# Grouping the batch loads and giving them more buffers in a fused attention, Fourier and gated MLP kernel

## The chip, the core and the metric

The kernel runs on one core of one Trainium2 chip. The metric is the device time of one execution in microseconds (us), as a median over several runs. A core has five engines that run side by side and meet through semaphores: PE (TensorE, matrix multiply, with PEld for its weight loads), DVE (VectorE), ACT (ScalarE), POOL (GpSimd) and SP (SyncE, which in this kernel issues every DMA).

## What is computed

The reference is three layers one after the other, for a batch of 4, a sequence of 1088 and a model width of 128 (4 heads of 32). Everything is in float32.

```python
# 1. linear attention with 64 product features per head
a, b = S1 @ x, S2 @ x                      # 8 + 8 numbers for each token and head, for x = q and x = k
phi = outer(a, b)                          # 64 features
kv, z = sum_s phi(k) v, sum_s phi(k)
attn = (phi(q) @ kv) / (phi(q) @ z + 1e-6)
# 2. Fourier mixing and a channel MLP
u = x + real(fft(fft(x, axis=seq), axis=feature))
x2 = u + relu(layernorm(u) @ w_ch1) @ w_ch2
# 3. a spatial gating unit
h = relu(x2 @ w_in); gate, v = halves of h
out = (gate * (w_spatial @ layernorm(v) + b_spatial)) @ w_out
```

The spatial product is the large one: a 1088 x 1088 matrix by 1088 x 512 in each of the 4 batches. The kernel gets float32 accuracy out of it by splitting both operands into a high and a low part, so that each product is three matmuls.

## The kernel before, in words

The program is written with a framework that takes the source as a list of operations with a priority, follows tiles and their buffers, and fixes an order for each engine at compile time. Operations that stand later in the source can therefore be put ahead of earlier ones on their engine, wherever the framework's own model has them ready first. At run time each engine follows its fixed order and waits on semaphores.

Each batch goes through these stages, and each stage has a function of its own:

- `keys(b)` (L355) handles the keys in three chunks of 384 tokens. For each chunk it loads the value tile `vx` (L359, 128 x 396 floats, 198 KB) and calls `feats`, then multiplies features by values into `kv` (L365), which ACT copies out to `kvz`.
- `feats` (L336) loads a chunk of transposed keys or queries (`kt` or `qt`, L338, 128 x 384 floats, 192 KB, both in the tag `kq` with 6 buffers), multiplies it by the projection `sb_s` on PE (L341, tile `abp`), copies that to `ab` on ACT (L343, 2 buffers) and forms the products of features `pp` on DVE (L347, 3 buffers of 128 x 768 floats).
- `queries(b)` (L376) does `feats` for three chunks of queries, transposes the products on PE (L386, tile `qps`, which needs the permutation tile `prm`), copies them to `qp` on ACT (L391), multiplies them by `kvz` on PE (L397, tile `nm`) and divides on DVE into `ub` (L405 to L407).
- `fourier_seq(b)` (L414) and `fourier_feat(b)` (L475) add the real part of the two-dimensional transform to `ub`. They need the tables `tr` (1096 KB), `trr` (137 KB) and `dd` (256 KB).
- `channel(b)` (L165) is the channel MLP and the first half of the gating unit, which leaves the normalised `v` as `vh` and `vlo` for the spatial product.
- `spatial(b)` (L570) is the spatial product (tile `ac`, L589 to L591) and the output.

The weights arrive in double precision, as ten blocks of 256 KB (`wraw`, L328): two each of w1, w2 and wo and four of wi. `weight` (L331) converts each with five DVE, four ACT and two POOL instructions. The spatial weights (`wst`, L126) come in strips of 192 KB and pass through buffers that are shared with later tiles. `warm(n)` (L505) issues n matmuls of zeros whose place in PE's order is fixed: 11 at the start, 10 early in the Fourier stage of batch 0 and 20 ahead of `channel(0)`.

The order of the loads in the source is, before the change: `sb_s`; then for batch 0 the pairs `vx`, `kt` of the three chunks; `prm`; four weight blocks (wi 0 and 1, wo 0 and 1; L526); the three `qt`; six weight blocks (w1, w2, wi 2 and 3; L528); `tr`, `trr`, `dd` (L531 to L533); the pairs of batch 1 and its `qt`; the spatial strips. The loads of batch 2 and batch 3 stand inside `keys` and `queries` in the loop at L556, behind the strips of the first two column blocks of the spatial weights.

Of the kernel before, what the change touches and what calls it, by code (L numbers as in the profile page):

```python
# [7 lines left out]
F32 = mybir.dt.float32  # L8
# [10 lines left out]
P = 128  # L19
# [46 lines left out]
def fourier_attention_gmlp_kernel(  # L66
# [18 lines left out]
    nc = tc.nc  # L85
# [8 lines left out]
    prm = const.tile([P, 3, P], F32, name="prm")  # L94
# [193 lines left out]
    ca = sa.enter_context(tc.tile_pool(name="ca", bufs=1, side="right"))  # L288
# [3 lines left out]
    tr = ca.tile([P, 2, 4, NCOL], F32, name="tr")  # L292
    trr = ca.tile([P, NCOL], F32, name="trr")
    dd = ca.tile([P, 2, 2, DM], F32, name="dd")
# [5 lines left out]
    def xtile(b, shape, name):  # L300
        if b == 0 and name not in ("abp", "nm"):
            return psy.tile(shape, F32, tag="acc", bufs=2, name=name)
        return psx.tile(shape, F32, tag="x", bufs=3, name=name)
# [21 lines left out]
    def weight_load(tag, *blocks):  # L325
        t = const.tile([P, len(blocks), 512], I32, tag=tag, name="wraw")
        for i, (n, src, k) in enumerate(blocks):
            nc.sync.dma_start(out=t[:, i, :], in_=src.bitcast(I32)[:, 512 * k:512 * k + 512])  # L328
            wraw[n, k] = t[:, i, :]

    def weight(n, k):  # L331
        w_ = from_f64(wraw.pop((n, k)), 256, None, False)
        A.copy(out=wt[n][:, k, 0, :], in_=w_)
        sub(G, wt[n][:, k, 1, :], w_, wt[n][:, k, 0, :])

    def feats(src, b, c, tag):  # L336
        x = ca.tile([P, 384], F32, tag="kq", bufs=6, name=tag)
        nc.sync.dma_start(out=x, in_=src[b, :, 384 * c:384 * c + 384])  # L338
        ap = xtile(b, [P, 2, 3, 32], "abp")
        for t in range(3):  # L340
            mm(out=ap[:, :, t, :], lhsT=x[:, 128 * t:128 * t + 128], rhs=sb_s, start=True, stop=True)  # L341
        ab = ca.tile([P, 2, 3, 32], F32, tag="ab", bufs=2, name="ab")
        A.copy(out=ab, in_=ap)  # L343
        pp = ca.tile([P, 12, 8, 8], F32, tag="pp", bufs=3, name="pp")
        a_ = ab[:, 0, :, :].rearrange("p t (h i) -> p (t h) i", h=4)
        b_ = ab[:, 1, :, :].rearrange("p t (h j) -> p (t h) j", h=4)
        (G if [b, tag[0], c] in [[3, 'k', 2]] else V).tensor_tensor(  # L347
            out=pp,
            in0=a_.unsqueeze(3).to_broadcast([P, 12, 8, 8]),
            in1=b_.unsqueeze(2).to_broadcast([P, 12, 8, 8]),  # L350
            op=ALU.mult,
        )
        return pp

    def keys(b):  # L355
        kv = psx.tile([P, 512], F32, tag="y", name="kv")[:, 0:66].rearrange("p (r d) -> p r d", r=2)
        for c in range(3):
            vx = ca.tile([P, 3, 4, 33], F32, tag="vx", bufs=3, name="vx")
            nc.sync.dma_start(out=vx, in_=vt[b, :, 3 * c:3 * c + 3, :, :])  # L359
            pp = feats(kT, b, c, "kt")  # L360
            for t in range(3):
                for pr in range(2):
                    for hh in range(2):
                        h = 2 * pr + hh
                        mm(  # L365
                            out=kv[64 * hh:64 * hh + 64, pr, :],
                            lhsT=pp[:, 4 * t + h, :, :].rearrange("p i j -> p (i j)"),
                            rhs=vx[:, t, h, :],
                            start=(c == 0 and t == 0 and pr == 0),
                            stop=(c == 2 and t == 2 and pr == 1),  # L370
                        )
        z = kvz[b % 2]
        A.copy(out=z[0:64, :, 0:33], in_=kv[0:64])
        A.copy(out=z[64:128, :, 33:66], in_=kv[64:128])

    def queries(b):  # L376
        z = kvz[b % 2]
        ub[b] = const.tile([P, NT, DM], F32, tag="ub", bufs=3, name="ub")
        qps = []
        for c in range(3):  # L380
            pp = feats(qT, b, c, "qt").rearrange("p t i j -> p (t i j)")
            qp = ca.tile([P, 2, 384], F32, tag="qp", bufs=3, name="qp")
            for pr in range(2):
                q_ = xtile(b, [P, 384], "qps")
                for t in range(3):
                    T.transpose(  # L386
                        out=q_[:, 128 * t:128 * t + 128],
                        in_=pp[:, 256 * t + 128 * pr:256 * t + 128 * pr + 128],
                        identity=ident,
                    )  # L390
                A.copy(out=qp[:, pr, :], in_=q_)  # L391
            qps.append(qp)
        for c, qp in enumerate(qps):
            nm = xtile(b, [P, 3, 4, 33], "nm")
            for t in range(3):
                for pr in range(2):
                    mm(  # L397
                        out=nm[:, t, 2 * pr:2 * pr + 2, :].rearrange("p h d -> p (h d)"),
                        lhsT=qp[:, pr, 128 * t:128 * t + 128],
                        rhs=z[:, pr, :],  # L400
                        start=True,
                        stop=True,
                    )
            rd = ca.tile([P, 3, 4, 1], F32, tag="rd", bufs=2, name="rd")
            V.tensor_scalar(out=rd, in0=nm[:, :, :, 32:33], scalar1=1e-6, scalar2=None, op0=ALU.add)  # L405
            V.reciprocal(out=rd, in_=rd)
            V.tensor_tensor(  # L407
                out=ub[b][:, 3 * c:3 * c + 3, :].rearrange("p t (h d) -> p t h d", h=4),
                in0=nm[:, :, :, 0:32],
                in1=rd.to_broadcast([P, 3, 4, 32]),  # L410
                op=ALU.mult,
            )
# [106 lines left out]
    blocks = [("w1", 0), ("w1", 1), ("w2", 0), ("w2", 1), ("wi", 2), ("wi", 3), ("wi", 0), ("wi", 1), ("wo", 0), ("wo", 1)]  # L519
    srcs = {"w1": w1, "w2": w2, "wi": win, "wo": wout}  # L520
    def load_raw(tag, part):
        weight_load(tag, *[(n, srcs[n], k) for n, k in part])

    keys(0)
    nc.sync.dma_start(out=prm, in_=perm)
    load_raw("wsh0", blocks[6:])  # L526
    queries(0)
    load_raw("wsl0", blocks[:6])  # L528
    weight("w1", 0)
    weight("w1", 1)  # L530
    nc.sync.dma_start(out=tr, in_=trig)  # L531
    nc.sync.dma_start(out=trr, in_=trig_r)
    nc.sync.dma_start(out=dd, in_=ddft)  # L533
    fourier_seq(0)
    fourier_feat(0)
    weight("wi", 2)
# [9 lines left out]
    for _ in channel(0, pre, psy, "acc", 2, psy, "o", None, [convert(("w2", 0), ("w2", 1), ("wo", 0), ("wo", 1)), None, None, None, convert(("wi", 0), ("wi", 1)), None]):  # L546
        pass
    keys(1)
    queries(1)
    with tc.issue_after(marks[0, 1, "t1"].ins):  # L550
        spatial_split(pre, 0, [G], spatial_load(const, 0, ring))
    sp.close()
# [2 lines left out]
    spatial_split(ca, 1, (V, G), spatial_load(pw, 1, ring))  # L555
    for b in range(1, B):  # L556
        if b > 1:
            keys(b)
            queries(b)
        fourier_seq(b)  # L560
        fourier_feat(b)
# [174 lines left out]
```

## Time and profile before

| | us |
|---|---|
| median of 3 runs | 468.57 |
| lowest and highest run | 465.99 and 468.98 |
| the profiled execution, whole | 467.55 |
| the profiled execution, its span | 465.7 |
| PE busy in the span | 444.4 |
| DVE busy in the span | 276.3 |
| ACT busy in the span | 192.3 |
| POOL busy in the span | 65.5 |

The span runs from the first to the last instruction that the profiler recorded; 1.85 us of the execution lie around it. Busy times are sums over the whole span, and the stages differ: the first 100 us hold the attention, the Fourier transform and the channel MLP of batch 0 and all weight conversions, and from then on PE also has the spatial product to work on. All matmuls are pipelined, so a PE that counts as busy can still be working slowly, at a lower granted clock or with short matmuls.

### The profile page before, as it was taken

The numbers are of one execution on the slowest core, as the hardware profiler recorded it, in microseconds if no ns is written. First come the engines' busy times: TensorE is split into PE (matmuls) and PEld (weight loads), VectorE is DVE, ScalarE is ACT, GpSimd is POOL, SyncE is SP. The second block draws the span as 40 slices with busy tenths as digits, with TensorE's granted clock in tenths as the row PEclk, the third lists the DMA queues.
The fourth block names the chain that finished last, engine by engine and source line by source line (L and its number), as shares of the span: only waits on it lengthen the run. The fifth ranks groups of instructions, "written<-read, shape, count | busy, mean of one in ns | idle before, by whom it ended". The sixth has DMA issues, their size and how long they took to land.

```text
span 465.7 us, 7498 instructions
## 1 busy us (share of the span) xinstructions
PE 444.4 (95%) x2893; PEld 410.0 (88%) x2893; DVE 276.3 (59%) x685; ACT 192.3 (41%) x448; POOL 65.5 (14%) x105
## 2 busy tenths in 40 slices
PE   8968898989999998999999999999999999999996
PEld 7847777868979788889999999999999999999995
DVE  3589998896564484878736273784454547221221
ACT  3546687464223153555524242563333335312221
POOL 2045394471100130000000000000000000000000
PEclk9799799999999998999999999999999999999999
DMA  8961143004000040000000000000000000000000
GB/s 245 374 205 34 35 121 106 16 19 129 27 1 1 2 144 1 0 1 18 16 1 0 1 17 1 18 1 14 1 1 18 0 2 18 14 1 17 1 17 15
DMA packets 13007, 19.29 MB, mean 41 GB/s; under 512 B 1446, under 2 KB 11436, under 8 KB 12844
## 3 DMA queue, kind: packets, MB, share of 16 engines
q1 hardware_dynamic: 12972, 18.82, 12.7%
q8 instruction: 23, 0.38, 0.3%
q14 instruction: 12, 0.10, 0.1%
HBM read 16.58 MB, written 2.23 MB: 40 GB/s over the span
## 4 chain that ended last, share of the span: by engine, by line
PE 71%; issue 9%; DVE 7%; ACT 5%; POOL 3%; DMA 3%; SPq 1%; POOLq 0%; DVEq 0%; ACTq 0%
PE ac L590 12%; PE ac L591 12%; PE ac L589 12%; PE v_ps L256 2%; PE dft L451 2%; PE v_ps L254 2%; PE c L227 2%; PE v_ps L255 2%; PE ac L597 1%; PE ac L596 1%; PE u_ps L582 1%; PE c L225 1%; PE u_ps L583 1%; PE u_ps L584 1%; PE c L226 1%
## 5 line engine op out<-in xcount | busy, mean ns | idle before, releaser
L589 PE MATMUL ac<-wsh,vh 128*128 128x384 f32 (+1 forms) x384 | 126.9, 331 | 0.6 <-ACT vh L270 0.6
L590 PE MATMUL ac<-wsl,vh 128*128 128x384 f32 (+1 forms) x384 | 126.9, 330 | 0.0
L591 PE MATMUL ac<-wsh,vlo 128*128 128x384 f32 (+1 forms) x384 | 126.6, 330 | 0.0
L590 PEld LDWEIGHTS ac<-wsl,vh 128*128 128x128 f32 x384 | 72.4, 189 | 1.8 <-issue 1.0
L589 PEld LDWEIGHTS ac<-wsh,vh 128*128 128x128 f32 x384 | 72.3, 188 | 1.6 <-ACT vh L270 0.9
L591 PEld LDWEIGHTS ac<-wsh,vlo 128*128 128x128 f32 x384 | 72.4, 188 | 0.9 <-issue 0.4
L600 DVE TENSOR_TENSOR uh<-ac,uh 128x384 f32<-128x384 f32 (+1 forms) x48 | 25.4, 530 | 55.3 <-PE ac L597 55.3
L586 ACT ACTIVATE uh<-u_ps 128x384 f32<-128x384 f32 (+1 forms) x48 | 22.6, 470 | 47.7 <-PE u_ps L584 45.0
L347 DVE TENSOR_TENSOR pp<-ab 128x768 f32<-128x768 f32 x23 | 25.2, 1108 | 18.9 <-ACT ab L343 17.6
L114 DVE TENSOR_TENSOR gl<-uh,gh 128x384 fp32r<-128x384 f32 (+1 forms) x48 | 26.2, 547 | 13.4 <-ACT gh L601 13.3
L245 POOL CAST xh<-xh 128x64 fp32r<-128x64 f32 x4 | 2.2, 541 | 202.7 <-ACT xh L242 202.7
L601 ACT CAST gh<-uh 128x384 fp32r<-128x384 f32 (+1 forms) x48 | 23.5, 492 | 15.0 <-DVE uh L600 14.8
L261 DVE BATCH_NORM_STATS2 bst<-vn 128x6 f32<-128x512 f32 x27 | 18.6, 693 | 16.8 <-ACT vn L259 16.7
L259 ACT ACTIVATE vn<-v_ps 128x512 f32<-128x512 f32 x27 | 16.0, 598 | 19.2 <-PE v_ps L256 18.7
L241 DVE TENSOR_TENSOR xt<-c,xt 128x384 f32<-128x384 f32 (+1 forms) x12 | 6.4, 532 | 27.8 <-PE c L227 27.8
L397 PE MATMUL nm<-kvz,qp 128*128 128x66 f32 x144 | 17.4, 278 | 0.0
L397 PEld LDWEIGHTS nm<-kvz,qp 128*128 128x128 f32 x144 | 17.3, 198 | 0.0
L282 ACT CAST vh<-vn 128x1024 fp32r<-128x1024 f32 x12 | 12.6, 1047 | 10.3 <-PE ac L590 8.2
L227 PE MATMUL c<-hl,w 128*128 128x384 f32 (+1 forms) x48 | 16.4, 342 | 0.3 <-DVE hl L220 0.3
L225 PE MATMUL c<-hh,w 128*128 128x384 f32 (+1 forms) x48 | 16.6, 346 | 0.0
L256 PE MATMUL v_ps<-wi,xl 128*128 128x512 f32 x36 | 15.3, 425 | 1.1 <-DVE xl L114 1.1
L582 PE MATMUL u_ps<-sxh,wi 128*128 128x384 f32 (+1 forms) x48 | 16.2, 338 | 0.0
(714 smaller groups left out, 950.2 us busy)
## 6 DMA issues: line engine op xcount, KB each, us to landing
wst<-in_wsp SPq DMA_DIRECT2D x18, 192.0 KB, 3.3
vx<-in_vt SPq DMA_DIRECT2D x12, 198.0 KB, 4.1
kt<-in_kT SPq DMA_DIRECT2D x12, 192.0 KB, 3.8
qt<-in_qT SPq DMA_DIRECT2D x12, 192.0 KB, 4.1
w2st<-in_wsp SPq DMA_DIRECT2D x9, 160.0 KB, 3.3
tr<-in_trig SPq DMA_DIRECT2D x1, 1096.0 KB, 8.9
wraw<-in_win SPq DMA_DIRECT2D x4, 256.0 KB, 5.4
wraw<-in_w SPq DMA_DIRECT2D x4, 256.0 KB, 4.8
```

Source lines behind the costliest of these rows:

```text
L114: eng.tensor_tensor(out=lo, in0=x, in1=hi.bitcast(F32), op=ALU.subtract)
L225: mm(out=c2[:, 0:n], lhsT=wpart("w2", 0, 128 * m, 128), rhs=hh[:, 0:n], start=(m == 0), stop=False)
L227: mm(out=c2[:, 0:n], lhsT=wpart("w2", 0, 128 * m, 128), rhs=hl[:, 0:n], start=False, stop=(m == 3))
L256: mm(out=h_, lhsT=xl[:, cs], rhs=wt["wi"][:, 2:4, 0, :], start=False, stop=True)
L347: (G if [b, tag[0], c] in [[3, 'k', 2]] else V).tensor_tensor(out=pp, in0=a_.unsqueeze(3).to_broadcast([P, 12, 8, 8]), in1=b_.unsqueeze(2) ...
L397: mm(out=nm[:, t, 2 * pr:2 * pr + 2, :].rearrange("p h d -> p (h d)"), lhsT=qp[:, pr, 128 * t:128 * t + 128], rhs=z[:, pr, :], start=True, ...
L586: A.activation(out=uh[:, 0:n], in_=h_[:, 0:n], func=ACTF.Relu)
L589: mm(out=ac[:, 0:n], lhsT=vh[:, k, ms], rhs=wsh[c][:, k, :], start=(k == 0), stop=False)
L590: mm(out=ac[:, 0:n], lhsT=vh[:, k, ms], rhs=wsl[c][:, k, :], start=False, stop=False)
L591: mm(out=ac[:, 0:n], lhsT=vl[:, k, ms], rhs=wsh[c][:, k, :], start=False, stop=False)
L600: V.tensor_tensor(out=uh[:, 0:n], in0=ac[:, 0:n], in1=uh[:, 0:n], op=ALU.mult)
L601: A.copy(out=gh[:, 0:n], in_=uh[:, 0:n])
```

## The change

All loads of a batch are taken out of `keys` and `feats` and put into a function `loads(b)`, which issues three `kt`, three `qt` and three `vx` in that order (for batch 0 with `prm` after the `kt`). `loads(0)` stands ahead of everything else, then come `tr`, `trr`, the six weight blocks w1, w2, wi 2 and 3, then `dd`, `loads(1)`, and last the four weight blocks wi 0 and 1, wo 0 and 1. `loads(2)` is moved ahead of the strips of the spatial weights, and `loads(3)` stands at the head of batch 3. The tag `kq` gets 10 buffers instead of 6, `vx` 5 instead of 3, and `pp` 4 instead of 3. The memory reserved by the `dynamic_dma_scratch_size` of the program goes from 4096 to 1024.

```diff
--- before.py
+++ after.py
@@ -333,15 +333,27 @@
         A.copy(out=wt[n][:, k, 0, :], in_=w_)
         sub(G, wt[n][:, k, 1, :], w_, wt[n][:, k, 0, :])
 
-    def feats(src, b, c, tag):
-        x = ca.tile([P, 384], F32, tag="kq", bufs=6, name=tag)
-        nc.sync.dma_start(out=x, in_=src[b, :, 384 * c:384 * c + 384])
+    loaded = {}
+
+    def loads(b):
+        for tag, src in (("kt", kT), ("qt", qT)):
+            for c in range(3):
+                x = loaded[b, tag, c] = ca.tile([P, 384], F32, tag="kq", bufs=10, name=tag)
+                nc.sync.dma_start(out=x, in_=src[b, :, 384 * c:384 * c + 384])
+            if b == 0 and tag == "kt":
+                nc.sync.dma_start(out=prm, in_=perm)
+        for c in range(3):
+            vx = loaded[b, "vx", c] = ca.tile([P, 3, 4, 33], F32, tag="vx", bufs=5, name="vx")
+            nc.sync.dma_start(out=vx, in_=vt[b, :, 3 * c:3 * c + 3, :, :])
+
+    def feats(b, c, tag):
+        x = loaded.pop((b, tag, c))
         ap = xtile(b, [P, 2, 3, 32], "abp")
         for t in range(3):
             mm(out=ap[:, :, t, :], lhsT=x[:, 128 * t:128 * t + 128], rhs=sb_s, start=True, stop=True)
         ab = ca.tile([P, 2, 3, 32], F32, tag="ab", bufs=2, name="ab")
         A.copy(out=ab, in_=ap)
-        pp = ca.tile([P, 12, 8, 8], F32, tag="pp", bufs=3, name="pp")
+        pp = ca.tile([P, 12, 8, 8], F32, tag="pp", bufs=4, name="pp")
         a_ = ab[:, 0, :, :].rearrange("p t (h i) -> p (t h) i", h=4)
         b_ = ab[:, 1, :, :].rearrange("p t (h j) -> p (t h) j", h=4)
         (G if [b, tag[0], c] in [[3, 'k', 2]] else V).tensor_tensor(
@@ -355,9 +367,8 @@
     def keys(b):
         kv = psx.tile([P, 512], F32, tag="y", name="kv")[:, 0:66].rearrange("p (r d) -> p r d", r=2)
         for c in range(3):
-            vx = ca.tile([P, 3, 4, 33], F32, tag="vx", bufs=3, name="vx")
-            nc.sync.dma_start(out=vx, in_=vt[b, :, 3 * c:3 * c + 3, :, :])
-            pp = feats(kT, b, c, "kt")
+            vx = loaded.pop((b, "vx", c))
+            pp = feats(b, c, "kt")
             for t in range(3):
                 for pr in range(2):
                     for hh in range(2):
@@ -378,7 +389,7 @@
         ub[b] = const.tile([P, NT, DM], F32, tag="ub", bufs=3, name="ub")
         qps = []
         for c in range(3):
-            pp = feats(qT, b, c, "qt").rearrange("p t i j -> p (t i j)")
+            pp = feats(b, c, "qt").rearrange("p t i j -> p (t i j)")
             qp = ca.tile([P, 2, 384], F32, tag="qp", bufs=3, name="qp")
             for pr in range(2):
                 q_ = xtile(b, [P, 384], "qps")
@@ -521,16 +532,17 @@
     def load_raw(tag, part):
         weight_load(tag, *[(n, srcs[n], k) for n, k in part])
 
+    loads(0)
+    nc.sync.dma_start(out=tr, in_=trig)
+    nc.sync.dma_start(out=trr, in_=trig_r)
+    load_raw("wsl0", blocks[:6])
+    nc.sync.dma_start(out=dd, in_=ddft)
+    loads(1)
+    load_raw("wsh0", blocks[6:])
     keys(0)
-    nc.sync.dma_start(out=prm, in_=perm)
-    load_raw("wsh0", blocks[6:])
     queries(0)
-    load_raw("wsl0", blocks[:6])
     weight("w1", 0)
     weight("w1", 1)
-    nc.sync.dma_start(out=tr, in_=trig)
-    nc.sync.dma_start(out=trr, in_=trig_r)
-    nc.sync.dma_start(out=dd, in_=ddft)
     fourier_seq(0)
     fourier_feat(0)
     weight("wi", 2)
@@ -547,6 +559,7 @@
         pass
     keys(1)
     queries(1)
+    loads(2)
     with tc.issue_after(marks[0, 1, "t1"].ins):
         spatial_split(pre, 0, [G], spatial_load(const, 0, ring))
     sp.close()
@@ -555,6 +568,8 @@
     spatial_split(ca, 1, (V, G), spatial_load(pw, 1, ring))
     for b in range(1, B):
         if b > 1:
+            if b > 2:
+                loads(b)
             keys(b)
             queries(b)
         fourier_seq(b)
@@ -719,7 +734,7 @@
     import concourse.bacc as bacc
     from concourse.bass_utils import run_bass_kernel_spmd
 
-    nc = bacc.Bacc("TRN2", target_bir_lowering=False, num_devices=1, dynamic_dma_scratch_size=4096)
+    nc = bacc.Bacc("TRN2", target_bir_lowering=False, num_devices=1, dynamic_dma_scratch_size=1024)
     lay = _layout(**{n: np.asarray(x) for n, x in inputs.items()})
     arrays, args = {}, []
     for n in _INS:
```

## Rows read from the trace of the kernel before

**Rows 1.** The page: busy time of PE and DVE in the span.
```profile
PE 444.4 (95%) x2893; PEld 410.0 (88%) x2893; DVE 276.3 (59%) x685; ACT 192.3 (41%) x448; POOL 65.5 (14%) x105
```

**Rows 2.** Windows: length, busy us (instructions) of PE, PEld, DVE, ACT, POOL; clock, DMA, GB/s.
```profile
26.00:60.00 34.00, 28.27 (x170) 22.30 (x170) 31.99 (x94) 20.54 (x51) 17.09 (x27) 0.90 0.24 79
60.00:88.00 28.00, 25.86 (x195) 22.11 (x194) 24.07 (x53) 19.56 (x46) 18.99 (x18) 1.00 0.34 94
88.00:180.00 92.00, 87.43 (x688) 74.38 (x688) 60.85 (x141) 34.09 (x85) 22.52 (x40) 0.98 0.14 41
180.00:466.00 286.00, 281.41 (x1670) 271.69 (x1668) 146.71 (x362) 107.32 (x239) 2.21 (x6) 1.00 0.02 8
```

**Rows 3.** The chain that ended last, its start: start us, length us, what.
```profile
2.59 4.22 DMA kt<-in_kT
6.82 5.74 DMA qt<-in_qT
12.70 3.46 PE abp L341 x18
```

**Rows 4.** Timeline of SP (DMA issues): start us, us spent issuing, engine, line, what, count.
```profile
4.49 0.91 SPq L328 DMA_DIRECT2D wraw<-in_win  x2
5.44 1.21 SPq L328 DMA_DIRECT2D wraw<-in_wout  x2
6.82 1.51 SPq L338 DMA_DIRECT2D qt<-in_qT  x3
...
13.01 0.36 SPq L531 DMA_DIRECT2D tr<-in_trig  x1
...
21.96 0.33 SPq L338 DMA_DIRECT2D kt<-in_kT  x1
...
73.59 7.16 SPq L338 DMA_DIRECT2D qt<-in_qT  x2
```

**Rows 5.** Waits of SP's own queue: who waited for whom, us in total, times, longest.
```profile
SPq L338 <- DMA tr<-in_trig: 4.0, 1, 4.0
```

**Rows 6.** Windows of the first 20 us, columns as in rows 2.
```profile
0.00:4.00 4.00, 2.43 (x6) 1.95 (x7) 1.77 (x11) 2.44 (x5) 3.19 (x13) 1.00 0.50 128
4.00:8.00 4.00, 3.96 (x20) 3.24 (x18) 0.48 (x2) 0.35 (x2) 0.00 (x0) 1.00 0.92 270
8.00:12.00 4.00, 3.29 (x78) 3.02 (x78) 2.35 (x3) 1.02 (x4) 0.00 (x0) 1.00 1.02 351
12.00:14.00 2.00, 1.30 (x9) 1.33 (x10) 0.01 (x1) 0.32 (x1) 0.00 (x0) 0.84 1.06 404
14.00:20.00 6.00, 6.00 (x31) 5.67 (x31) 4.74 (x11) 3.46 (x9) 0.00 (x0) 0.50 1.00 384
```

**Rows 7.** Timeline of DVE: start us, busy us, what, count [idle before <- released by].
```profile
7.65 2.70 DVE L347 TENSOR_TENSOR pp<-ab 128x768 f32<-128x768 f32 x3 [3.52 <-ACT ab L343]
13.99 0.96 DVE L347 TENSOR_TENSOR pp<-ab 128x768 f32<-128x768 f32 x1 [3.64 <-ACT ab L343]
...
16.55 0.96 DVE L347 TENSOR_TENSOR pp<-ab 128x768 f32<-128x768 f32 x1 [0.32 <-ACT ab L343]
...
24.49 1.01 DVE L407 TENSOR_TENSOR ub<-nm,rd 128x384 f32<-128x384 f32 x2
```

**Rows 8.** Timeline of PE: the warming matmuls, first projections, first spatial products.
```profile
1.57 5.06 PE L508 MATMUL wp<-a 128*128 128x512 f32 x11 [1.57 <-DVE a L503]
6.43 0.83 PE L341 MATMUL abp<-sb_s,kt 128*128 128x64 f32 x6
...
20.64 3.46 PE L397 MATMUL nm<-kvz,qp 128*128 128x66 f32 x30
...
86.75 0.42 PE L589 MATMUL ac<-wsh,vh 128*128 128x384 f32 x1
```

**Rows 9.** Timeline of DVE, as rows 7: a feature product of batch 1, then batch 2's first.
```profile
59.22 1.77 DVE L347 TENSOR_TENSOR pp<-ab 128x768 f32<-128x768 f32 x1
...
107.51 2.80 DVE L347 TENSOR_TENSOR pp<-ab 128x768 f32<-128x768 f32 x3
```

## The prediction

> **What bounds the kernel now.** Start with the page's busy times. PE is busy for 444.4 of 465.7 us, DVE for 276.3 [rows 1], so PE looks like the limit, with at most 21 us to win. The windows by stage show where those 21 us lie [rows 2]: from 180 us on PE idles for 4.6 of 286 us, between 88 and 180 us for 4.6 of 92. No load order helps there. Between 26 and 60 us it is DVE that is full, 31.99 of 34 us, and PE idles for 5.7; between 60 and 88 us DVE is busy for 24.1 of 28. In these two stages batch 0 goes through the Fourier transform and the channel MLP beside the weight conversions, and at their end, at 86.75 us, the spatial product begins to run in earnest [rows 8], which then fills every gap of PE. So the kernel is a start-up of some 87 us, then PE's sum. A microsecond taken out of the start-up should come out of the total, because the work behind it stays the same.
>
> Read next the start of the chain of waits [rows 3]. Its links up to 12.7 us are two transfers: a key chunk that lands at 6.81 and a query chunk that lands at 12.56 us. SP's timeline tells why the second is so late [rows 4]: four weight blocks (1 MB) were put into the queue at 4.49 to 6.65 us, ahead of the queries at 6.82. DVE shows what that costs [rows 7]: it finishes the three feature products of the keys at 10.35 us, then idles 3.64 us until those of the queries start at 13.99. These should follow at once; instead they end at 17.51, and `ub` is complete at 25.50.
>
> **When the loads land after the change.** The windows of the first 20 us give the rate [rows 6]: 0.51 MB (millions of bytes) have moved by 4 us, 1.59 by 8, 3.00 by 12, 3.80 by 14. Two known landings set the delay behind this curve [rows 3]. The second key chunk ends 0.86 MB of the queue, which the curve reaches at 5.3 us; it landed at 6.81. The first query chunk ends 2.71 MB, reached at 11.2 us; it landed at 12.56. So I add 1.5 us. In the new order the last `kt` ends 0.66 MB, the last `qt` 1.44, the last `vx` 2.05, `tr` 3.17 and the second w1 block 3.84 MB. That gives landings at 6.0, 8.9, 10.8, 13.9 and 15.6 us. The same bytes go through the same queue; only their order changes.
>
> **The keys: nothing won, nothing lost.** Their projections cannot start before PE has run its 11 warming matmuls, whose place is fixed and which last until 6.63 us; the first starts at 6.43 already today [rows 8]. So the key products still run from about 7.65 to 10.35. The values come later than before, at 9.5 to 10.8 us, but `kv` is needed only when the first transposed queries are ready, after 12 us. Bounds: nothing, to 0.8 us if PE's order puts the last `kv` group ahead of a query projection.
>
> **The queries: 4.3 us won.** With `qt` on chip at 8.9 us and a fourth `pp` buffer (the second query product takes over the first key chunk's buffer, which `kv` frees at about 10.3), the three query products follow the keys on DVE: 10.35 plus 3 x 0.96 is 13.2 us, against 17.51 [rows 7]. From the last product to the complete `ub` it took 25.50 - 17.51 = 8.0 us. I keep those 8.0 us, so `ub` is ready at 21.2, 4.3 us earlier. For the tail the bounds are wide: the clock was at 0.50 between 14 and 20 us [rows 6], that is at 1.2 instead of 2.4 GHz, and it had fallen after 12 to 14 us, where PE had worked only 1.30 of 2 us while it waited for `qt`. At full clock 30 of the 36 `nm` matmuls took 3.46 us [rows 8], so all 36 take 4.2; started when the first queries are transposed, at about 12.8, they end at 17.0, and 1.2 us of division makes `ub` complete at 18.2, a gain of 7.3. With all 36 at half clock they take 8.3 and `ub` comes at 22.3, a gain of 3.2. The 8.0 us that were measured lie nearer to the second.
>
> **Transformation tables and weights: 0.** `tr` is needed at the start of the transform, now about 24 us, and lands at 13.9. The w1 blocks land by 15.6, ahead of the end of the queries. The late weight blocks and the loads of batch 1 are held up in another way. A `kt` load waited 4.0 us on `tr` [rows 5], and it was the eighth DMA behind `tr` (issued at 21.96 [rows 4], when `tr` had just landed). So an issue here waits for the landing of the DMA eight places before it. In the new order that is `dd`, which waits until 13.9, and with it `loads(1)` and the last four blocks. All bytes ahead of the spatial strips are the same as before, so all have landed by about 26 us; their first users come after 38 us. If this cover were gone, they could cost the 4 us of the wait itself.
>
> **Batch 2 and 3: 0, bounded by -2 and +5.** The queries of batch 2 were issued at 73.59 us and after [rows 4], while DVE formed their first product only at 107.51 [rows 9]. So that load was not what batch 2 waited for, and bringing it forward wins nothing by itself. The 2 us are a part of what PE idles between 60 and 88 us; the 5 us are the rival below. The smaller scratch has no user in the trace: every DMA is issued on SP's queue, none on POOL's. I put it at 0.
>
> **The sum.** DVE is full from 26 to 60 us, so its work starts 4.3 us earlier and ends 4.3 us earlier, as does the start of the spatial product. The span becomes 465.7 - 4.3 = 461.4, the profiled execution 467.55 - 4.3 = 463.25. The median of the runs stands 1.0 above that execution, which would make it 464.3. I name 463.5.
>
> **Rival 1, the clock holds.** PE no longer waits for queries between 11.3 and 12.7 us, the clock stays at its upper level, and `ub` gains 7.3 us: 460.2 us. For it speaks that the fall came directly behind that gap; against it that PE's work there stays thin, made of short bursts paced by DVE. The Trainium skill (TensorE: Matmul & The Clock Gate, HAM oscillation) names this case: waits for DMAs between bursts throttle the array again, and the next burst starts slow. The trace agrees on the order of events; the rule alone would give the 460.2.
>
> **Rival 2, the lead is lost.** The 4.3 us reach 26 us but not the end, because the stage from 60 to 88 us is not bound by DVE alone (3.9 us of idle time there) and its fixed orders wait for other things, such as the spatial strips, whose buffers come free no sooner. Then 466 to 469, say 467.5.
>
> **Rival 3, slower.** `loads(2)` now makes batch 2 ready far earlier in the framework's model, which may put its six feature products on DVE ahead of the last normalised `v` of batch 0. One takes 0.96 us in an idle core and 1.77 in this crowded stage [rows 7, 9]; I take 1.5, so six are 9 us in a stage where DVE has under 4 us to spare. The spatial product would start 9.0 - 4.3 = 4.7 us later than today: 472. It decides from the third product that goes ahead. Against it speaks that batch 2 stands behind batch 0 in priority, and that even its keys, loaded long before, waited until 107.51.
>
> That the change does nothing of what it says can be ruled out as far as the loads go, since SP's order of today follows the source.
>
> **How the numbers follow.** The forecast (gain of 2 to 6.5 us) gets 0.44, rival 1 0.26, rival 2 0.17, rival 3 0.13. A measurement of this kernel tells about 1% from no change, here 4.7 us. Four tenths of the forecast's range and all of rival 1 lie beyond that: 0.18 + 0.26 = 0.44 for faster. The rest of the forecast and rival 2 are no change that can be told: 0.26 + 0.17 = 0.43. Rival 3 is the 0.13 for slower. The range runs from 457 (rival 1 with the 2 us of batch 2 and a run's spread) to 470.5 (short of rival 3); the likeliest case alone spans 461 to 466.
>
> **What would show it.** Right: `qt` issued before 5 us, DVE's six first products in one run from 7.65 to about 13.3, `ub` complete by 22 us, the first dense `ac` near 82 us. The clock between 14 and 20 us tells the forecast from rival 1. DVE products of batch 2 before 80 us show rival 3. I am wrong if `ub` is early and the spatial product is not, or if the key products start late because `kt` or `sb_s` did.

## The result, and the profile after

| | before | after |
|---|---|---|
| median, us | 467.83 (465.99 to 468.98, 4 runs) | 462.45 (462.09 to 463.2, 4 runs) |
| profiled execution, whole | 467.55 | 462.66 |
| its span | 465.7 | 460.7 |
| ratio of the times | | 0.9891, 95% interval 0.9853 to 0.9929 |

The changed kernel is faster by 1.1% (0.7 to 1.5%), about 5 us; 463.5 was forecast. It was timed again in a later series beside three variants: 462.32, ratio 0.9879 (0.9836 to 0.9921). The size is right. The way the gain reaches the end is not the one that was forecast, and most of this part is about that.

First the rows that answer to those of before. The page's line on PE, and the windows of the start and by stage (columns as in rows 2); line numbers have moved, L338 to L342, L347 to L359, L365 to L376, L397 to L408, L493 to L504, L591 to L606:

```profile
PE 441.3 (96%) x2893; PEld 405.5 (88%) x2893; DVE 276.4 (60%) x685; ACT 191.7 (42%) x448; POOL 68.4 (15%) x105
```

```profile
12.00:14.00 2.00, 1.71 (x28) 1.43 (x25) 1.04 (x2) 1.28 (x4) 0.00 (x0) 1.00 1.02 388
14.00:20.00 6.00, 5.06 (x47) 4.89 (x45) 2.37 (x11) 3.48 (x8) 0.00 (x0) 1.00 1.05 379
26.00:60.00 34.00, 27.90 (x192) 20.84 (x192) 30.42 (x90) 20.29 (x53) 15.55 (x19) 0.80 0.41 136
60.00:88.00 28.00, 26.50 (x158) 22.62 (x157) 24.58 (x60) 19.48 (x45) 21.45 (x27) 1.00 0.26 72
88.00:180.00 92.00, 87.89 (x698) 74.72 (x697) 61.21 (x137) 35.59 (x88) 22.51 (x34) 1.00 0.10 28
```

Against [rows 6], the granted clock stays at 1.00 (2.4 GHz) from 12 to 20 us, where it had fallen to 0.50 (1.2 GHz). Against [rows 2], it is lower from 26 to 60 us, 0.80 where it was 0.90. This fall has moved, not gone; another stretch of some 6 us at 0.50 stands in both, at 48 to 54 us before and 51 to 57 after. DVE is busy for 30.42 of the 34 us from 26 to 60, where it was for 31.99.

The timelines of SP, of DVE and of PE at the start show that the loads did what the change says:

```profile
1.17 1.37 SPq L342 DMA_DIRECT2D kt<-in_kT  x3
2.58 0.43 SPq L344 DMA_DIRECT2D prm<-in_perm  x1
3.06 1.38 SPq L342 DMA_DIRECT2D qt<-in_qT  x3
...
13.28 0.33 SPq L539 DMA_DIRECT2D dd<-in_ddft  x1
13.66 2.32 SPq L342 DMA_DIRECT2D kt<-in_kT  x3
```

```profile
7.31 3.56 DVE L359 TENSOR_TENSOR pp<-ab 128x768 f32<-128x768 f32 x4 [3.19 <-ACT ab L355]
11.21 1.83 DVE L359 TENSOR_TENSOR pp<-ab 128x768 f32<-128x768 f32 x2 [0.34 <-PE kv L376]
...
19.92 0.55 DVE L418 TENSOR_TENSOR ub<-nm,rd 128x384 f32<-128x384 f32 x1
...
27.05 1.82 DVE L359 TENSOR_TENSOR pp<-ab 128x768 f32<-128x768 f32 x2
```

```profile
10.21 2.29 PE L376 MATMUL kv<-vx,pp 128*64 128x33 f32 x72
12.43 0.87 PE L397 MATMUL qps<-prm,pp 128*128 128x128 f32 x6
...
15.59 3.46 PE L408 MATMUL nm<-kvz,qp 128*128 128x66 f32 x30
20.62 0.46 PE L429 MATMUL rp<-ub,prm 128*128 128x128 f32 x2 [1.56 <-DVE ub L418]
20.83 2.56 PE L519 MATMUL wp<-a 128*128 128x512 f32 x10
23.22 2.12 PE L353 MATMUL abp<-sb_s,kt 128*128 128x64 f32 x18
```

The queries are issued at 3.06 us instead of 6.82 [rows 4]. DVE forms its six first products without the gap of 3.64 us [rows 7], ending at 11.21 + 1.83 = 13.04. `ub` of batch 0 is complete at 19.92 + 0.55 = 20.47, 5.0 us earlier. The last line of each of DVE and PE was not in the forecast: the projections of batch 1's keys (23.22, 18 matmuls are three chunks) and batch 1's first feature products (27.05) now run inside batch 0's Fourier stage. Before, a product of batch 1 still stood at 59.22 [rows 9].

Following the same events through both timelines gives the lead at each point (starts of the event, us; for `ub` its end):

| event | before | after | after minus before |
|---|---|---|---|
| `ub` of batch 0 complete | 25.50 | 20.47 | -5.0 |
| Fourier stage of batch 0, last `ub<-urm` | 39.23 | 41.81 | +2.6 |
| last three normalised `v` of batch 0 | 94.38 | 94.31 | -0.1 |
| last `ub` of batch 1 out of the division | 88.94 | 81.95 | -7.0 |
| Fourier stage of batch 1 | 107.31 | 101.32 | -6.0 |
| Fourier stage of batch 2 | 136.39 | 133.78 | -2.6 |
| Fourier stage of batch 3 | 165.24 | 163.33 | -1.9 |
| first `un` of the channel MLP of batch 1 | 175.39 | 172.54 | -2.85 |
| first `v_ps` matmul behind it | 187.08 | 182.09 | -5.0 |
| end of the span | 465.7 | 460.7 | -5.0 |

A second profile of the changed kernel has 41.30, 100.61, 162.62, 171.82 and 181.36 us for its Fourier stages of batches 0, 1 and 3, the first `un` and the first `v_ps`, and a span of 459.9. So a single row can move by 0.7 us or so between two executions of one kernel, and smaller differences between rows tell nothing. Stretches between two rows repeat better: from the end of batch 3's Fourier stage to the first `un` it is 9.21 and 9.20 us.

So batch 0's lead of 5.0 us is gone, and turned round, by 42 us: batch 1's work now stands ahead of it. Batch 1 is ahead until 101 us; where PE is full (62.17 of the 64 us from 100 to 164 before, 62.53 after) it shrinks to about 2. The last 2 to 3 us come from another place, between 164 and 184 us, which the prediction had not looked at. There the rows of before, DVE, POOL and PE of the timelines:

```profile
174.47 0.88 POOL L114 TENSOR_TENSOR wr<-w2st,bh 1x320 fp32r<-1x320 f32 x1
```

```profile
175.39 0.86 DVE L195 TENSOR_SCALAR un<-ub,mv,r 128x128 f32<-128x128 f32 x3 [0.29 <-POOL wr L114]
```

```profile
175.88 0.30 PE L199 MATMUL t<-prm,un 128*128 128x128 f32 x1 [2.07 <-DVE un L195]
```

and, of before, the windows:

```profile
172.00:174.00 2.00, 1.81 (x11) 1.50 (x9) 1.93 (x4) 1.82 (x5) 1.90 (x3) 1.00 0.09 32
174.00:176.00 2.00, 0.12 (x1) 0.15 (x2) 1.67 (x6) 0.87 (x2) 1.28 (x2) 1.00 0.00 0
176.00:178.00 2.00, 2.00 (x13) 1.97 (x13) 2.00 (x6) 0.89 (x3) 0.00 (x0) 0.80 0.03 8
178.00:180.00 2.00, 2.00 (x8) 2.00 (x7) 0.00 (x0) 0.00 (x0) 0.00 (x0) 0.50 0.00 0
```

After the change the same place, PE's timeline and then the windows:

```profile
173.02 0.30 PE L199 MATMUL t<-prm,un 128*128 128x128 f32 x1 [0.92 <-DVE un L195]
```

```profile
172.00:174.00 2.00, 1.08 (x9) 1.01 (x9) 1.48 (x5) 0.20 (x1) 0.20 (x1) 1.00 0.00 0
174.00:176.00 2.00, 2.00 (x13) 1.77 (x12) 1.25 (x4) 0.87 (x3) 0.00 (x0) 1.00 0.04 8
178.00:180.00 2.00, 2.00 (x14) 2.00 (x13) 0.56 (x1) 0.49 (x1) 0.00 (x0) 1.00 0.00 0
```

Read it as a seam: three batches' preparation is over, the strips of the last spatial column block (tile `w2st`) are split on ACT, DVE and POOL, and the normalised `un` of batch 1's channel MLP waits behind the last split. PE runs dry for 2.07 us before and 0.92 after. Before, the clock then falls to 0.50; over 176 to 184 us its mean is 0.79, which costs 8 x 0.21 = 1.7 us of a full PE; after, it stays at 1.00. Together 1.15 + 1.7 = 2.85 us. With the 1.9 us of the Fourier stage of batch 3 that is 4.75, close to the 5.0 of the span. The table closes the sum: 1.91 us up to the end of that stage, 0.94 more up to the first `un`, 2.14 more up to the first `v_ps`, together 4.99. Behind that matmul nothing is won: from there the span lasts 278.6 us before and after, and 278.5 to 279.4 in all twelve profiles of this record.

```profile
187.08 0.45 PE L254 MATMUL v_ps<-wi,xh 128*128 128x512 f32 x1
```

```profile
182.09 0.45 PE L254 MATMUL v_ps<-wi,xh 128*128 128x512 f32 x1
```

The first line is of before, the second of after. What the larger buffers do at this seam shows in SP's waits. Before, the `w2st` strips were issued at 165.11 us behind a wait for batch 3's last matmuls `urm`; after, at 144.35 behind batch 3's projections `abp`. The program puts `w2st` into memory that the pool of the earlier stages has released, and with other buffer counts its strips wait for other tiles. What this is worth is read below. Of the waits of SP's queue, before and then after:

```profile
SPq L126 <- PE urm L493: 5.8, 1, 5.8
```

```profile
SPq L126 <- PE abp L353: 37.3, 1, 37.3
```

### The profile page after: what moved, and what is told of

It reads as the page before. It is cut to its first block, busy times and chain, and to the rows that moved or that the text cites. A ratio compares the mean times of both kernels' runs of the same rounds, so it can differ in the third digit from the quotient of the medians.

```text
span 460.7 us, 7484 instructions
## 1 busy us (share of the span) xinstructions
PE 441.3 (96%) x2893; PEld 405.5 (88%) x2893; DVE 276.4 (60%) x685; ACT 191.7 (42%) x448; POOL 68.4 (15%) x105
## 4 chain that ended last, share of the span: by engine, by line
PE 77%; issue 9%; DVE 9%; ACT 3%; POOL 1%; POOLq 0%; DVEq 0%; ACTq 0%
PE ac L605 12%; PE ac L604 12%; PE ac L606 12%; PE dft L462 3%; PE v_ps L254 2%; PE v_ps L256 2%; PE c L225 2%; PE c L227 2%; PE c L226 2%; PE v_ps L255 2%; PE nm L408 2%; PE ac L612 2%; PE ac L611 1%; PE u_ps L597 1%; PE u_ps L598 1%
## 5 line engine op out<-in xcount | busy, mean ns | idle before, releaser
L606 PE MATMUL ac<-wsh,vlo 128*128 128x384 f32 (+1 forms) x384 | 126.3, 329 | 2.2 <-POOL vlo L114 2.2
L606 PEld LDWEIGHTS ac<-wsh,vlo 128*128 128x128 f32 x384 | 72.0, 188 | 3.3 <-POOL vlo L114 3.1
L359 DVE TENSOR_TENSOR pp<-ab 128x768 f32<-128x768 f32 x23 | 23.7, 1062 | 11.8 <-ACT ab L355 11.4
L408 PE MATMUL nm<-kvz,qp 128*128 128x66 f32 x144 | 17.4, 271 | 0.0
L408 PEld LDWEIGHTS nm<-kvz,qp 128*128 128x128 f32 x144 | 17.2, 192 | 0.1
L242 ACT CAST xh<-xt 128x384 fp32r<-128x384 f32 (+1 forms) x12 | 6.0, 497 | 26.0 <-DVE xt L241 26.0
```

Source lines behind the costliest of these rows:

```text
L408: mm(out=nm[:, t, 2 * pr:2 * pr + 2, :].rearrange("p h d -> p (h d)"), lhsT=qp[:, pr, 128 * t:128 * t + 128], rhs=z[:, pr, :], start=True, ...
L606: mm(out=ac[:, 0:n], lhsT=vl[:, k, ms], rhs=wsh[c][:, k, :], start=False, stop=False)
```

## The experiments

All ratios are to the kernel before, run beside each variant, with 95% intervals. One fact about the programs helps to read them: in the traces, the instructions on PE, DVE, ACT and POOL stand in exactly the order of before when only the buffers are larger, and in exactly the changed kernel's order when only the order of the loads is new. So the two halves of the change separate cleanly: one changes the order, the other what that order waits for.

**Buffers only.** The kernel before, with the new counts and the smaller scratch. The changed arguments, in short:

```diff
-tag="kq", bufs=6   tag="vx", bufs=3   tag="pp", bufs=3   dynamic_dma_scratch_size=4096
+tag="kq", bufs=10  tag="vx", bufs=5   tag="pp", bufs=4   dynamic_dma_scratch_size=1024
```

> Loads in their old order and place; only the buffers (10, 5, 4) and the smaller scratch of the change. Every compute engine keeps the order of the kernel before. Theory A (two separate gains: about 2.7 us at the start from the load order, about 2.4 us near 170 us because the larger pool of the first stage lets the strips of the last spatial column block load earlier): 465.4 us against 467.8, the w2st strips issued near 147 us instead of 165.1, PE's idle time between 172 and 176 us down from 2.1 us to about 1, the clock between 176 and 182 us at 1.00. Theory B (the whole gain is the early queries, the buffers cost and give nothing): 467.8 us, within 0.5.

Measured: 465.89 us, ratio 0.9978 (0.9958 to 0.9999). The start is as before (Fourier stage of batch 0 ends at 39.55). The `w2st` strips are issued at 142.50, PE's gap at the seam is 1.79 us, and the clock behind it does not fall:

```profile
172.00:176.00 4.00, 2.21 (x14) 1.92 (x13) 3.90 (x10) 1.64 (x5) 2.96 (x3) 1.00 0.00 0
176.00:184.00 8.00, 8.00 (x48) 7.97 (x49) 4.21 (x11) 3.29 (x8) 0.00 (x0) 1.00 0.01 2
```

Theory A had the strips and the clock, but PE's gap is hardly smaller than the 2.07 us of before. So the buffers are worth 0.2% (1 us) by themselves, and what they gain is found at the seam, not at the loads they were added for. Counts and scratch were not tried apart.

But the early strips are not what brings that microsecond. The first `un` starts at 175.44 us, as before (175.39), 9.91 us behind the end of batch 3's Fourier stage instead of 10.15. What is won lies behind it: from the first `un` to the first `v_ps` it takes 10.16 us instead of 11.69, because the clock stays up. The single executions agree. Of the 66 executions of the kernel before that were timed beside the variants, 23 had a mean granted clock of 0.983 or more, with a median of 466.07 us; the other 43 have a median of 468.06. With the larger buffers 11 of 12 executions had such a clock, and the median is 465.85. So the buffers by themselves save hardly any work; executions with a low clock become rarer, and why is not shown. All ten executions of the changed kernel had 0.983 or more, and their median is 462.36. By this rough split 3.7 us of the change's 5 remain at a like clock, and about 1.3 come from the clock.

**Order only.** The changed kernel with the old counts (the diff above turned round).

> The loads in the new order, the buffers as before (6, 3, 3) and the old scratch. Every compute engine has the order of the changed kernel. Theory A: 465.1 us, ub of batch 0 complete near 20.5 us, the w2st strips issued only near 162 us, and the fall of the clock near 176 us still there. Theory B: 462.5 us, like the changed kernel.

Measured: 464.94 us, ratio 0.9951 (0.9928 to 0.9975). The start is that of the changed kernel (`ub` at 20.01, Fourier stage of batch 0 at 41.14, of batch 1 at 100.46); the strips go out at 162.62, as late as before. Theory A had the time, but not the fall of the clock: PE's gap at the seam is 2.27 us, longer than the 2.07 of before, and yet the clock from 172 to 184 us is 1.00:

```profile
173.76 0.30 PE L199 MATMUL t<-prm,un 128*128 128x128 f32 x1 [2.27 <-DVE un L195]
```

```profile
176.00:184.00 8.00, 8.00 (x45) 7.47 (x44) 4.09 (x8) 3.56 (x9) 0.00 (x0) 1.00 0.00 0
```

The two halves give 0.22 and 0.49%, together 0.71; the whole gave 1.09 and 1.21. Their intervals overlap with a plain sum, and with a small surplus as well. The traces speak for a surplus. With the new order, the first `un` follows the end of batch 3's Fourier stage by 10.53 us when the strips are late and by 9.21 (9.20 in the second profile) when they are early, so early strips are worth 1.3 us there; with the old order they were worth 0.24.

**Queries first.** Of the new order, only the part the forecast was built on: batch 0's queries ahead of the first weight blocks. (`load_x` is the load taken out of `feats`.)

```diff
+    for c in range(3):
+        early[0, "qt", c] = load_x(qT, 0, c, "qt")
     load_raw("wsh0", blocks[6:])
     queries(0)
```

> The kernel before with one edit: the three query loads of batch 0 go ahead of the four weight blocks of wi and wo. Buffers as before. The engines keep batch 0 ahead of batch 1, nearly in the order of the kernel before. Theory B: ub of batch 0 at about 21.5 us instead of 25.5, every later stage of batch 0 some 4 us earlier, 463.6 us. Theory A: the lead reaches the end of the normalised v of batch 0 (95.5 us before), but the seam near 172 us is as it was: 464 to 465. If neither holds, and the lead is spent between 26 and 95 us, 467.5.

Measured: 465.64 us, ratio 0.9957 (0.9938 to 0.9975). Here batch 0's `ub` is complete at 21.3, 4.2 us early, and no feature product of batch 1 comes ahead of the transform. Still the lead is only 2.7 us when the transform begins (`eo` at 23.07 against 25.75), 2.2 at the end of the Fourier stage (37.06 against 39.23) and 2.7 at the last normalised `v` (91.63 against 94.38). The first loss is in DVE's order: five instructions of weight conversions (1.8 us) stand ahead of `eo`. The second goes with the clock: PE is nearly idle from 24 to 28 us, and from 30 us on the transform's matmuls run at half clock and take 0.66 us instead of 0.39:

```profile
24.00:26.00 2.00, 0.69 (x4) 0.19 (x2) 1.89 (x6) 0.43 (x1) 1.92 (x6) 1.00 0.90 277
26.00:28.00 2.00, 0.20 (x1) 0.00 (x0) 1.92 (x4) 0.77 (x2) 1.08 (x2) 1.00 1.03 348
...
30.00:32.00 2.00, 2.00 (x12) 1.32 (x10) 2.00 (x7) 1.10 (x3) 0.73 (x1) 0.50 0.11 35
```

What is left at 37 us does arrive: the lead is 2.8 us at the end of batch 1's Fourier stage (104.54), 2.7 at that of batch 3 (162.53), and 2.7 at the end of the span (463.0). At the end of batch 3's Fourier stage this kernel is as far as the changed one (163.33 and 162.62); the changed kernel is ahead only behind the seam, where this one has late strips (162.40), a gap of 2.19 us and a fall of the clock behind it.

**Queries first, with the buffers.** Both edits above on the kernel before.

> The one edit of queries_first together with the larger buffers and smaller scratch. Theory A: 2.4 us less than queries_first, so 461.5 to 462.5, with the w2st strips issued near 145 us. Theory B: the same as queries_first within 0.5 us.

Measured: 464.59 us, ratio 0.9952 (0.9924 to 0.9981); strips at 140.83, clock 1.00 behind the seam. The median is 1.05 us below queries first, between the two theories, and the ratios can't be told apart. Against the 0.9879 (0.9836 to 0.9921) of the changed kernel timed again, what is left of the change (the rest of the order) is worth another 0.7% beside the buffers, though the two intervals all but touch. That timing again had this expectation:

> The changed kernel without any edit, timed beside the others on one chip. Every theory: 462.5 us against 467.5, ratio 0.989.

**Batch 1's loads put back.** The changed kernel, with `loads(1)` behind the late weight blocks:

```diff
     nc.sync.dma_start(out=dd, in_=ddft)
-    loads(1)
...
+    loads(1)
     keys(1)
```

> The changed kernel with one edit: loads(1) is issued just ahead of keys(1), behind all other early loads. The framework then places the Fourier stage of batch 0 ahead of the kv products of batch 1, which the changed kernel has the other way round. Theory A1 (the lead of the queries is worth more to batch 0 than the early work of batch 1): Fourier stage of batch 0 complete near 37.5 us instead of 41.8, last normalised v near 92 instead of 95.8, and 461 us. Theory A2 (PE's filling work decides, and batch 1 ahead is what fills it): batch 1's ub late, near 86 instead of 81.4 us, the lead near 104 us at most 2.8 us as in queries_first, and 463 to 464.

Measured: 467.17 us, ratio 0.9984 (0.9954 to 1.0014). Both theories missed the time: nearly the whole gain is gone. The keys of batch 1 are issued 3.4 us later (17.07 against 13.66), and batch 1's projections stay ahead of batch 0's transform in PE's order. Those of its keys still run at 23.18, but those of its queries wait until 28.49 behind the copies `ab`, and the transform stands behind them. It ends 1.3 us earlier than in the changed kernel all the same (Fourier stage of batch 0 at 40.52), 3 us later than theory A1 had it. PE's waits between 22 and 36 us, then windows of this kernel:

```profile
PE abp L353 <- ACT ab L355: 3.2, 1, 3.2
```

```profile
24.00:26.00 2.00, 1.30 (x12) 1.16 (x11) 1.93 (x6) 0.00 (x0) 1.69 (x4) 1.00 1.05 354
26.00:28.00 2.00, 0.00 (x0) 0.00 (x0) 1.01 (x5) 1.53 (x4) 0.00 (x0) 1.00 1.05 371
28.00:30.00 2.00, 0.43 (x2) 0.30 (x2) 1.53 (x2) 1.58 (x6) 0.96 (x2) 0.76 1.06 374
30.00:32.00 2.00, 1.40 (x4) 0.54 (x6) 2.00 (x7) 0.88 (x2) 0.75 (x2) 0.50 1.06 378
```

DVE idles too, 1.01 us busy of 26 to 28. What is late is batch 1, as theory A2 had it: its last `ub` is complete at 87.03 us (81.95 in the changed kernel) and its Fourier stage ends at 104.68 instead of 101.32. Batch 0's last `v` stands at 95.93. The strips go out early (145.15) and yet PE's gap at the seam is 2.32 us and the clock falls (0.80 from 176 to 184): early strips alone don't close the seam. Since the edit moves the load and the order at once, it doesn't give a price for either.

**Batch 2's loads put back** to the head of batch 2 in the loop.

> The changed kernel with one edit: loads(2) stays at the head of batch 2 in the loop, where it was before the change, behind the spatial strips. All compute engines keep the order of the changed kernel. Theory A and B alike: the products of batch 2 do not wait for their loads, so 462.5 us, within 0.7. Rival: batch 2's keys start later than 103.9 us because their loads stand behind the strips, which wait until about 100 us, and the time rises by what they start later, 2 to 4 us.

Measured: 462.9 us, ratio 0.9889 (0.9846 to 0.9931), the same as the changed kernel. That part of the change is worth nothing that these runs can tell. The engines' orders are those of the changed kernel, and this profile will be of use once more below.

**Queries first, less work on DVE.** One of the five DVE instructions of each weight conversion is left out.

```diff
-        V.tensor_scalar(out=x, in0=hi_, scalar1=0xFFFFF, scalar2=0x100000, ...)
+        if fast:
+            V.tensor_scalar(out=x, in0=hi_, scalar1=0xFFFFF, scalar2=0x100000, ...)
+        else:
+            x = hi_
```

> queries_first, with the masking of the high words (one DVE instruction of 0.28 us for each of the ten weight blocks) left out, so the mantissas of the weights are not those of the reference; the order of the engines changes a little. Theory D (DVE is the limit between ub of batch 0 and the end of its Fourier stage, because weight conversions that the old queries wait had hidden now stand there, and so a lead of 4.2 us shrinks to 2.2): Fourier stage of batch 0 complete 1 to 2 us before the 37.3 us of queries_first, the last normalised v 2 to 3 us before 92.1, total 462.5 to 463.5. Rival (a chain through PE and ACT sets that stage, the clock's fall near 30 us with it): no earlier than 36.8 us, total within 0.7 of 465.6.

Measured: 464.3 us, ratio 0.993 (0.9898 to 0.9963). The Fourier stage of batch 0 ends at 37.02, as with queries first alone (37.06). So DVE's load alone is not what holds that stage, against the reading of [rows 2] that DVE sets the pace there. The edit also shifts the order a little, and the clock fell once more than in queries first (0.50 from 24 to 26 us), so it doesn't show what holds the stage in DVE's place.

**More warming matmuls.** Is it the clock, then? 24 warming matmuls instead of 10 keep PE busy over its idle stretch, in the kernel with the queries first, and 20 instead of 10 in the changed kernel.

```diff
         if b == 0:
-            warm(10)
+            warm(24)
```

> The kernel with only batch 0's queries put forward, and 24 instead of 10 warming matmuls of zeros at the head of batch 0's Fourier stage, so that PE has work until about 28 us, where it idled for most of 24 to 28 us. Theory K (the fall of the clock at 30 to 33 us is what shrank the lead of the queries from 4.2 to 2.2 us): the granted clock stays at 1.00 through 26 to 36 us, the dft matmuls keep 0.39 us, the Fourier stage of batch 0 (last ub<-urm) ends at about 36.0 instead of 37.06, and the time is about 464.6 instead of 465.6. Rival O (the order and the chain of DVE instructions set the stage): the clock holds and the stage still ends within 0.3 us of 37.06, the time within 0.5 us of 465.6. Rival C (the longer warming keeps the first dft waiting): the stage ends after 37.3.

> The changed kernel with 20 instead of 10 warming matmuls at the head of batch 0's Fourier stage. The order behind them shifts a little, since the framework schedules around the longer warming: 21 instead of 36 matmuls of kv stand ahead of the first dft. Theory K (PE's gap at 26 to 28 us lets the clock fall to 0.50 at 30 to 36, which costs the Fourier stage about 2 us): clock 1.00 there, last ub<-urm of batch 0 at about 39.5 instead of 41.8, total about 460.5. Rival O (batch 1's keys ahead of it set its end, the clock has only a small share): the stage ends after 41 us and the total stays at 462 to 463. Rival C (the warming puts off batch 1's keys on PE and with them the DVE work behind them): the total is above 463.

Measured, queries first with 24: 472.57 us, ratio 1.0113 (1.0079 to 1.0146), some 7 us slower than with 10. At first the clock does what it should: it stays at 1.00 until 36 us, the transform's matmuls take 0.39 us and are done at 32.18 + 0.62 = 32.8 us instead of 34.4 (33.79 + 0.62). But in the order that the framework made for the longer warming, conversions of a weight block stand ahead of the step behind the transform (the copy `tb`) on ACT. PE, ACT and DVE of this kernel's timelines:

```profile
32.18 0.62 PE L459 MATMUL dft<-trr,lrb 128*64 128x274 f32 x2
34.85 1.13 PE L488 MATMUL ups<-dd,tb 128*128 128x256 f32 x4 [2.04 <-ACT tb L480]
```

```profile
34.02 0.51 ACT L314 ACTIVATE dy<-dy,cst 128x256 int32<-128x256 int32 x1
34.43 0.36 ACT L480 COPY tb<-dft 128x274 f32<-128x274 f32 x1
```

```profile
37.76 0.41 DVE L318 SCALAR_TENSOR_TENSOR ds<-dy,ds 128x256 int32<-128x256 int32 x1
38.10 0.68 DVE L496 TENSOR_TENSOR ub<-ups,ub 128x512 f32<-128x512 f32 x1
```

In queries first the first `tb` starts at 32.59; here at 34.43, and the stage ends at 41.10 instead of 37.06. Not all of that is the order: behind PE's two waits for `tb` the clock falls after all (0.72 from 36 to 38 us, 0.50 from 38 to 42), and the second four `ups` matmuls take 2.07 us instead of 1.13. Batch 1's Fourier stage ends at 111.30 instead of 104.54, which is nearly the whole 7 us.

The changed kernel with 20: 464.31 us, ratio 0.9936 (0.9912 to 0.9961), some 0.5% above both timings of the changed kernel, with intervals that overlap a little; clock 1.00 from 26 to 42 us, Fourier stage of batch 0 at 42.12 (41.81). Rival C has it: batch 1's Fourier stage ends at 104.34 instead of 101.32.

Both edits rewrite the order. The kernel with batch 2's loads put back has the changed kernel's own order, and in its profile the clock fell earlier, during the warming matmuls, and was 1.00 from 26 to 42 us. The end of its transform and the matmuls behind it, then the end of the transform in the changed kernel:

```profile
35.95 0.62 PE L462 MATMUL dft<-trr,lrb 128*64 128x274 f32 x2
37.58 1.13 PE L491 MATMUL ups<-dd,tb 128*128 128x256 f32 x4 [1.01 <-ACT tb L483]
```

```profile
38.41 0.62 PE L462 MATMUL dft<-trr,lrb 128*64 128x274 f32 x2
```

The transform is done 2.5 us earlier, and PE then waits for `tb`. From batch 0's first `eo` to the end of its Fourier stage it takes 18.58 us, and 19.4 to 19.6 in the three profiles of the same order in which the clock fell at about 30 us (after, its second profile, order only). So the clock's price is real, 1.6 us in the transform of queries first and 2.5 here, but only about 1 us of it reaches the end of the stage; the rest is set by the fixed order.

## Why the prediction was right in size and wrong in its way

- **What bounds the kernel.** Right that the work ahead of PE's full stage is what can be won. Wrong that this is one start-up of 87 us: there is a second seam at 164 to 184 us. The stage of 88 to 180 us in [rows 2], 4.6 us idle with a clock of 0.98, was dismissed with "no load order helps there"; 2.85 us came out of its end and the first 4 us behind it. The "at most 21 us to win" counts idle time alone; what PE loses while it is busy at the lower clock, 1.7 us at this seam, is not in it.
- **Landings and keys.** Right as far as they can be checked: the key products run from 7.31, values delay nothing, and the first query product follows them. Six products ended at 13.04, forecast 13.2. The fifth product waited 0.34 us for its buffer, as the fourth buffer's reasoning allows.
- **The tail of the queries.** Forecast 8.0 us, measured 20.47 - 13.04 = 7.4. The gain became 5.0 instead of 4.3.
- **Rival 1** had its condition (clock 1.00 from 12 to 20 us) and not its price: 5.0 instead of 7.3 us. It had the `nm` matmuls run in one go from the time when the first queries are transposed, at 12.8. But PE's order runs all 72 `kv` matmuls first (to 12.50), and transposes, copies and `nm` then alternate; the run of 30 starts at 15.59. Its 3.46 us were right. One stage later the clock did fall: in the changed kernel PE is busy for 0.01 us of 26 to 28, waiting for DVE's products, and the granted clock is 0.93 from 28 to 30 and 0.50 from 30 to 36. The Trainium skill (TensorE: Matmul & The Clock Gate, HAM oscillation) says that a wait between bursts throttles the array again, there a wait for a DMA. This row agrees with it, but not every wait here did that: in the kernel before, PE waited 2.00 us ahead of its matmuls at 31.30, and the clock stayed at 1.00.
- **The table, weight and batch 2 loads at 0.** Right; batch 2's was tested. The wait for the DMA eight places before is there as forecast: `dd` waited 2.5 us on `tr`, and was issued at 13.28 (forecast 13.9).
- **The sum, the step that failed.** "DVE is full from 26 to 60 us, so its work starts 4.3 us earlier and ends 4.3 us earlier" did not hold. Even with the queries alone put forward, 4.2 us became 2.2 by 37 us, with less work on DVE as well; in the changed kernel batch 0 lost its lead by 42 us. That DVE was busy 94% was true, but it followed an order with conversions of weights in it, and what stood late was what the order put late. The other half of the step, that a lead at the end of the start-up comes out of the total, did hold with the queries alone: 2.2 us at 37 us, 2.7 at the end. The spatial product's first `ac` came at 79.21 against 80.20, its dense part not earlier: from 84 to 92 us PE is busy for 6.05 us, where it was for 7.96, and between 76 and 100 us it runs 38 `ac` matmuls, where it ran 41. An early `ub` and a spatial product that is not early is the sign of being wrong that the prediction named.
- **Rival 3** had the right mechanism with the wrong batch and sign: the early loads did bring a later batch ahead of batch 0's work on DVE, batch 1 instead of 2. Batch 0 paid for it. That batch 1's lead is what the seam needed is not shown: at the end of batch 3's Fourier stage, queries first, without that lead, is as far as the changed kernel.
- **Rival 2** (467.5) is what the lead of batch 0 did, without the two other gains. So the figure came out close partly by luck: a forecast lead of 4.3 that didn't arrive, and 5.0 from 1.9 us of later batches and some 3 us at a seam not in the sum.

How the 1.9 us at the end of batch 3's Fourier stage divide between batch 1's early keys and the clock was not settled, nor was the reason why the clock falls at the seam in some executions and not in others.

## What to carry to other kernels

Where a framework derives the engines' order from the source and the loads, moving a load is two changes, its time and the order of its consumers; list the order of each engine before pricing the load. A busy engine carries a lead through only if the critical work is what stands next in its order, so follow a lead event by event rather than by busy shares. And count the later seams, where PE runs dry for a microsecond or two between blocks, with a possible fall of the clock behind it. Buffer counts can change what happens there without any change in the engines' order: here they moved the last strips from 165 to 143 us.

## What the runs showed of the hardware that was not expected

- A gap of PE can cost more than itself, and its length didn't tell whether it would. At the seam, gaps of 2.07 us (before), 2.19 (queries first) and 2.32 (batch 1's loads put back) were followed by a clock of 0.50; gaps of 2.27 (order only), 2.14 (24 warming matmuls), 2.00 (less work on DVE) and 1.79 (larger buffers) were not. With the fall it took 11.2 to 11.7 us from the first `un` to the first `v_ps`, without it 9.5 to 10.2. These are one profile each.
- The same program got a different clock from execution to execution: over the 66 timed executions of the kernel before, the mean granted clock ran from 0.972 to 0.989 and the time from 470.9 to 463.5 us.
- The clock fell with a delay: in queries first PE was nearly idle from 24 to 28 us, ran a first burst at 1.00, and was at 0.50 only from 30 us on, when it was busy without a break.
